# Seven half-size products for the last batch's first MLP product, and a first pair loaded in halves

## The chip, the cores and the metric

The kernel runs on one core of one Trainium2 chip. The metric is the device time of one execution in microseconds (us). It is 278.86 us before the change: the median of three runs that lie between 278.41 and 279.77.

A core has five engines that work side by side, each through its own instructions in order: TensorE (PE in the profile; PEld is its loading of weights), VectorE (DVE), ScalarE (ACT), GpSimd (POOL) and SyncE (SP), which here only issues transfers. They wait for each other by semaphores. PE writes its results to PSUM, a memory of eight banks; DVE and ACT read them there. Everything else lies in SBUF.

## The reference

Four batches of 768 positions go through an attention with 8 heads of 64 columns and then through a mixing layer with an MLP.

```python
# attention: blocks of 64 keys, each query keeps its 3 best blocks and its own
k_rep = k.reshape(B, H, n_blocks, block, D).mean(axis=3)
gate_scores = einsum('bhsd,bhnd->bhsn', q, k_rep)        # causal by blocks
sel = top 3 blocks of gate_scores, and the own block
attn = softmax(scale * q @ k.T, masked by sel and causality)
x = attn @ v                                             # (B, 768, 512)
# mixing
u = x + real(fft(fft(x, axis=1), axis=2))
un = (u - mean(u)) / sqrt(var(u) + 1e-6)
out = u + maximum(un @ w_ch1, 0) @ w_ch2                 # 512 -> 2048 -> 512
```

## The kernel before, in words

The eight heads of a batch are taken in four pairs, so there are 16 pairs, `P` = 0 to 15, and four batches, `b` = 0 to 3. The text `ORDER` names every step of the program once, as `step:arguments@place`. The `place` picks one of four PSUM tiles of two banks each, or one of a few buffers. A `~` ahead of a step puts it on the other of its two possible engines. The loop at the end walks through `ORDER`, and `WORK` gives the function of each step; the engines take their instructions in just this order. Nothing is rearranged at run time.

A pair's steps: `Lq`, `Lk`, `Lv` load q, k and v (SP). `tq` and `tk` (`a_tp`, L314) turn q and k on PE for pairs 0 to 6; for the first pair `tj` (`b_tp`, L323) turns k's last two of six row tiles. `qc` copies q in full precision, `qs` and `kc` write the f16 copies from which scores are made, `ks` and `kj` sum k by blocks. `g`, `gt`, `gx`, `gl`, `gm` (and `gj`, `tg`, `xg`, `lg`, `mg` for the first pair's second part) make the gate scores, turn them, find the third largest, compare (into `lt`) and turn the mask back (into `mt`). `s` are the scores, `e` the exponentials on ACT (L549), `d` the causal masks on POOL (L555), `v` the product with v, `x` its division by the sums.

A batch's steps: `fs`, `fd`, `f` fold the rows, `y` and `m` are the two transforms, `u` adds them to x (L691). `bn` takes mean and variance of each row tile (L747), `nv` guesses the inverse root, `nr` refines it on POOL, `xu` scales, and `un` turns the result by transposing transfers (L742) into `unT`, 512 columns on 4 x 128 partitions by 768 positions.

The MLP: `w:b,it` (L795) is one of 16 tiles of the first product; it takes four slices of 128 of the 512 inner columns, each by a matmul of 512 and one of 256 positions (L801, L803). `r` is its maximum with 0, into `hT` (L811 on DVE, L813 on ACT). In batches 0 and 1 `c` is the second product (L820) and `o` adds it to `u` (L826).

In batches 2 and 3 (`W7`) the second product is made by seven half-size products in place of eight. `T` makes four sums of parts of `w_ch2` in `w2t`, `S:b,i,n` (`h_comb`, L850) makes four sums of parts of `hT` per tile pair `i`, `p:b,n,st` (`w7_mm`, L863) is product `n` for row tile `st`, accumulated over `i`, and `po` (L886) adds PSUM to one or another quarter of `u`. Only two banks per row tile are used: product `n` goes on top of what the bank holds, and `po` reads the bank between products:

```python
W7_BANK = (0, 1, 0, 1, 1, 0, 0)
W7_FIRST = (True, True, False, True, False, False, False)
W7_OUT = ((0, 0), (0, 0), (0, 1), (1, 1), (0, 1), (1, 1), (1, 0))
```

`od` stores rows of `u`. `consts_first` (L896) issues the first pair's loads, makes the constants, and runs eight matmuls of zeros (L914).

Of the kernel before, what the change touches and what calls it, by code (L numbers as in the profile page):

```python
# [19 lines left out]
S = 768  # L20
# [96 lines left out]
e:3,5@1 d:2,2 x:1 s:3,2@0 e:3,0 Lq:6@0 d:3,5 g:5@1 vc:2 e:3,2 s:3,3@2 gt:5 Lk:6@1 d:2,1 gm:4@0
s:3,1@3 d:3,0 gu:5 s:3,4@1 e:3,3 gx:5 d:2,5 v:2@0 d:3,2 kb:7 LT:0 e:3,1 W:0 Lq:7@1 fs:1,0 ~go:5
e:3,4 s:4,4@2 x:2 d:3,1 s:4,2@3 d:3,3 e:4,4@0 s:4,0@1 d:3,4 gl:5 v:3@0 fs:2,0 gm:5@1 e:4,2 fs:2,1
fs:1,1 e:4,0 s:5,2@2 x:3 s:4,5@3 e:5,2@1 s:4,1@1 fd:2,1 s:4,3@0 fs:3,0 e:4,5 s:5,3@2 fs:3,1 e:4,1  # L120
fd:2,0 s:5,5@3 fd:3,1 e:5,5 tq:6@1 fd:3,0 e:4,3 ~fe:0,3 s:5,0@3 f:0,2 e:5,3 tk:6@0 ~fe:0,0 ~fe:0,2
f:0,0 ~qc:6@0 s:5,4@2 LF:0 f:0,1 fe:0,1 ks:6 e:5,4 y:0,0@1 qs:6 Lv:4@0 f:0,3 e:5,0 Lc:0 pg:0 ks:7
d:4,0 g:6@2 d:4,1 ty:0,0 d:4,2 y:0,1@3 gt:6 Lv:5@1 d:4,5 ~tr:0,0 d:5,2 gu:6 gx:6 Lk:8@2 d:4,3
s:5,1@2 W:1 go:6 gl:6 ~tr:0,1 qc:7@1 m:0,2@1 vc:4 ty:0,1 gm:6@2 d:4,4 kc:6 m:0,0@3 d:5,0 u:0,2@0
d:5,4 e:5,1 Lk:9@1 d:5,3 v:4@0 qs:7 u:0,0@1 xu:0,2 s:6,4@1 xv:0,2 x:4 vc:5 m:0,1@2 kh:7 e:6,4@0
d:5,5 s:6,1@3 u:0,1@2 d:5,1 s:6,3@0 e:6,1 xt:0,2@1 ~xu:0,0 g:7@2 xv:0,0 ~xu:0,1 v:5@3 e:6,3 gt:7
un:0,2 ~gu:7 W:2 ~xv:0,1 xt:0,0@2 s:6,5@1 un:0,0 xt:0,1@0 e:6,5 s:6,0@1 un:0,1 Lq:9@2 s:6,2@2 e:6,0
x:5 w:0,8@0 d:6,0 bn:0,0 w:0,1@1 r:0,8 gx:7 kc:7 go:7 w:0,5@3 gl:7 gm:7@3 K:7 kb:8 w:0,6@0 r:0,5
ks:8 r:0,1 bn:0,3 w:0,3@3 r:0,6 d:6,3 bn:0,5 e:6,2 w:0,12@1 r:0,3 Lq:8@0 s:7,5@0 s:7,0@2 ~r:0,12
e:7,5@1 s:7,4@3 kh:8 e:7,0 s:7,3@0 fs:4,1 w:0,0@1 qc:9@0 e:7,4 Li:0 Lv:6@0 kb:9 e:7,3 w:0,10@2 qs:9  # L130
Lv:7@1 bn:0,1 r:0,0 s:7,1@3 Lk:10@0 r:0,10 ks:9 d:7,3 w:0,11@0 e:7,1 qc:8@1 s:7,2@1 kh:9 ~r:0,11
d:7,1 w:0,7@2 e:7,2 d:6,2 d:7,0 fs:5,1 d:6,4 ~qs:8 g:8@3 X:0 g:9@0 gt:8 w:0,14@1 gu:8 d:7,4 gx:8
r:0,7 d:6,5 ~go:8 kc:9 w:0,9@3 X:1 gl:8 gt:9 gu:9 gm:8@0 d:6,1 d:7,5 w:0,2@2 r:0,14 ~r:0,9 Lk:12@1
d:7,2 vc:7 ~vc:6 gx:9 w:0,13@0 K:8 kc:8 kb:10 w:0,4@1 ~r:0,13 r:0,2 ks:10 v:7@3 r:0,4 ~go:9 gl:9
gm:9@1 K:9 s:8,3@0 x:7 s:8,1@2 v:6@1 e:8,1@1 bn:0,2 e:8,3 s:8,0@3 x:6 d:8,1 w:0,15@2 e:8,0 fs:5,0
fs:6,1 s:9,4@0 fs:7,1 r:0,15 fs:7,0 s:8,2@1 fs:4,0 s:8,4@3 e:9,4@0 fd:7,1 c:0,0,0@2 fs:6,0 fd:6,0
e:8,4 fd:7,0 e:8,2 bn:0,4 s:9,3@0 s:9,1@3 fd:6,1 kc:10 s:9,0@1 Lq:10@1 nv:0 c:0,0,1 ~fe:1,1 f:1,2
nr:0 f:1,3 e:9,3 f:1,1 ~fe:1,2 c:0,1,0 fe:1,0 f:1,0 fe:1,3 kh:10 e:9,1 Lv:9@1 kb:12 Lk:11@2 e:9,0
s:9,5@0 c:0,1,1 ks:12 e:9,5 y:1,0@3 o:0,1 Lq:11@2 qc:10@0 y:1,1@1 ~tr:1,0 o:0,0 qs:10 Lq:12@0
g:10@0 ~tr:1,1 c:0,4,0@2 gt:10 gu:10 kb:11 ty:1,0 d:8,2 d:9,5 gx:10 ty:1,1 d:8,0 m:1,2@0 od:0,1  # L140
d:9,1 Lq:13@1 ~go:10 d:9,0 c:0,5,0 u:1,2@3 vc:9 d:8,3 gl:10 ks:11 s:9,2@3 Lk:13@0 m:1,1@1 qc:11@1
kh:11 kh:12 xu:1,2 s:8,5@0 c:0,5,1 gm:10@2 u:1,1@4 K:10 kc:11 Lv:8@0 od:0,0 qc:12@0 c:0,4,1 e:8,5
e:9,2 ~xv:1,2 un:1,2 bn:1,3 pg:1 d:8,4 xu:1,1 g:12@1 d:9,3 g:11@0 d:8,5 c:0,2,0@3 ~qs:11 gt:11
d:9,4 o:0,5 gu:11 gx:11 od:0,5 xv:1,1 un:1,1 m:1,0@0 o:0,4 ~go:11 ~qs:12 gl:11 c:0,3,0 gt:12
gm:11@3 u:1,0@1 K:11 ~vc:8 c:0,3,1 gu:12 gx:12 xu:1,0 kc:12 d:9,2 v:8@2 o:0,3 ~go:12 ~xv:1,0 un:1,0
s:11,3@1 x:8 s:11,4@0 e:11,3@1 c:0,2,1 Lq:14@2 bn:1,4 e:11,4 bn:1,1 s:10,4@2 o:0,2 s:11,2@1 v:9@0
Lk:14@2 qc:13@1 e:11,2 fs:8,1 w:1,15@3 x:9 e:10,4@0 s:10,0@1 bn:1,5 r:1,15 od:0,3 s:10,2@2 od:0,4
gl:12 s:11,0@0 kb:13 e:10,2 w:1,10@3 Lk:15@1 bn:1,2 e:11,0 w:1,2@2 fs:8,0 e:10,0 ~r:1,10 s:11,1@0
gm:12@0 Lv:11@1 kb:14 K:12 s:10,1@1 e:11,1 w:1,4@3 ks:13 Lv:10@0 r:1,2 fs:9,1 s:10,3@0 e:10,1 ks:14
w:1,6@2 d:10,0 kh:13 ~r:1,4 d:11,2 kh:14 e:10,3 d:11,3 w:1,5@1 qc:14@0 r:1,6 s:10,5@3 w:1,12@0  # L150
~r:1,5 qs:13 e:10,5 kb:15 s:11,5@2 g:13@3 e:11,5 vc:11 g:14@1 r:1,12 gt:13 w:1,13@2 fs:9,0 kc:13
~gu:13 Lv:15@1 d:11,4 gx:13 d:10,2 od:0,2 s:12,0@3 d:11,0 bn:1,0 w:1,9@0 d:10,3 r:1,13 ~go:13
# [24 lines left out]
po:2,0,1 p:2,1,2 u:3,2@4 un:3,1 p:2,1,1 S:2,1,1 po:2,1,2 p:2,1,0 po:2,1,1 S:2,1,3 p:2,2,2 S:2,5,3
# [19 lines left out]
def kernel(  # L197
# [649 lines left out]
    def w2t_at(m, i0, i1):  # L847
        return w2t[m // 2][:, m % 2, i0:i1, :]
# [163 lines left out]
```

## Time and profile before

| | us |
|---|---|
| median of three runs | 278.86 |
| lowest and highest | 278.41, 279.77 |
| the profiled execution's own time | 277.79 |
| its span, first to last instruction | 276.1 |
| PE busy | 267.9 |
| DVE busy | 221.5 |
| ACT busy | 178.3 |
| POOL busy | 107.4 |

The profile is one execution. A row of a list of groups names the source line, the engine, the operation, what it writes and reads, how often it ran, its busy time in us, the mean time of one in ns, and how long the engine was idle ahead of it and for whom. A row of the timeline or of the chain of waits begins with its start and its length in us. A row by stretches has the stretch, its length, and the busy time and number of instructions of PE, PEld, DVE, ACT and POOL, and then the clock that PE was granted (1.00 is all of it), the share of the transfers and GB/s. PE's matmuls overlap in the pipeline: the length of one is longer than the time from one to the next.

### The profile page before, as it was taken

Reading aid. Unit: us, or ns where it says so; the run is one execution under the profiler, and the core shown is the slowest. Engines: PE = TensorE matmul, PEld = TensorE weight load, DVE = VectorE, ACT = ScalarE, POOL = GpSimd, SP = SyncE. Lnnn points to the kernel's source line nnn. Section 1 sums busy time; section 2 is a strip of 40 time slices with the busy share of each in tenths; the row PEclk is TensorE's granted clock in tenths of the full one; section 3 lists DMA queues with packets and bytes.
Section 4 is the critical chain, followed back from the end, with each engine's and each line's share of the span. In section 5 each row is a group of like instructions: output and inputs, shape, how many; then the busy total and the mean of one; then the engine's idle time right before and its main releaser. Section 6 shows DMA issues by size and latency. Waiting matters only on the chain.

```text
span 276.1 us, 7004 instructions
## 1 busy us (share of the span) xinstructions
PE 267.9 (97%) x2660; PEld 181.2 (66%) x2660; DVE 221.5 (80%) x683; ACT 178.3 (65%) x243; POOL 107.4 (39%) x304
## 2 busy tenths in 40 slices
PE   8899989999999999999999999999999999999995
PEld 4566766765576565666665755655766888666884
DVE  1888999998789889899789797879999894307883
ACT  3799999969999759978799687802546310274100
POOL 5155927634783476405976691520100011000000
PEclk9999999999999999999999999999999999999999
DMA  8999999998799999479471202351100412300025
GB/s 190 271 229 235 186 233 207 180 153 151 134 174 189 168 188 194 115 124 234 119 149 29 57 2 78 77 105 51 38 2 0 59 19 68 127 0 2 0 112 194
DMA packets 121138, 33.47 MB, mean 121 GB/s; under 512 B 113616, under 2 KB 118160, under 8 KB 121104
## 3 DMA queue, kind: packets, MB, share of 16 engines
q1 hardware_dynamic: 115872, 28.43, 48.1%
q0 software_dynamic: 3664, 4.19, 9.8%
q10 hardware_dynamic: 1568, 0.39, 0.6%
q8 instruction: 21, 0.34, 0.5%
q14 instruction: 13, 0.11, 0.1%
HBM read 28.55 MB, written 6.29 MB: 126 GB/s over the span
## 4 chain that ended last, share of the span: by engine, by line
PE 81%; DVE 6%; ACT 5%; POOL 2%; issue 2%; SPq 2%; DMA 1%; DVEq 0%; ACTq 0%; POOLq 0%
PE h L801 19%; PE cw L879 13%; PE c L820 12%; PE h L803 9%; PE sc L532 7%; PE av L567 5%; PE tp L320 2%; ACT pt L549 2%; PE yp L639 2%; PE sc L527 2%; PE mx L672 2%; SPq L742 2%; PE mx L673 2%; PE sc L539 1%; PE warmps L914 1%
## 5 line engine op out<-in xcount | busy, mean ns | idle before, releaser
L549 ACT ACTIVATE pt<-sc 128x1024 f16<-128x1024 f32 (+1 forms) x96 | 83.4, 925 | 12.1 <-PE sc L532 8.1
L801 PE MATMUL h<-unT,w 128*128 128x512 f16 x256 | 84.6, 379 | 0.3 <-DMA unT<-x 0.3
L803 PE MATMUL h<-unT,w 128*128 128x256 f16 x256 | 69.7, 272 | 0.0
L813 ACT ACTIVATE hT<-h 128x768 f16<-128x768 f32 x50 | 39.4, 811 | 41.1 <-PE h L803 40.7
L555 POOL TENSOR_SCALAR_AFFINE_SELECT pt<-pt 128x256 f16<-128x256 f16 x96 | 37.4, 413 | 21.0 <-ACT pt L549 19.9
L820 PE MATMUL c<-w_sb,hT 128*128 128x512 f16 x192 | 44.5, 379 | 0.0
L801 PEld LDWEIGHTS <-w 128*128 128x128 f16 x256 | 25.0, 98 | 29.7 <-issue 1.4
L820 PEld LDWEIGHTS <-hT 128*128 128x128 f16 x192 | 18.3, 98 | 20.3 <-issue 0.5
L253 POOL TENSOR_SCALAR_AFFINE_SELECT qk<-mt 32x160 f16<-32x160 f16 x72 | 23.9, 353 | 18.2 <-DVE mt L504 16.7
L803 PEld LDWEIGHTS <-w 128*128 128x128 f16 x256 | 25.0, 98 | 3.6
L532 PE MATMUL sc<-qk 96*128 96x512 f16 (+3 forms) x144 | 26.1, 305 | 0.0
L567 PEld LDWEIGHTS <-pt 128*128 128x128 f16 x672 | 22.3, 97 | 3.2 <-ACT pt L549 0.7
L567 PE MATMUL av<-v,pt 128*128 128x65 f16 x672 | 23.2, 193 | 0.3 <-ACT pt L549 0.3
L253 POOL TENSOR_SCALAR_AFFINE_SELECT qk<-q 64x768 f16<-64x768 f32 (+1 forms) x15 | 12.3, 822 | 22.8 <-ACT q L239 15.3
L886 DVE SCALAR_TENSOR_TENSOR u<-cw,rt,u 128x256 f32<-128x256 f32 x35 | 16.6, 480 | 4.7 <-PE cw L879 4.1
L879 PEld LDWEIGHTS <-s 128*128 128x128 f16 x192 | 18.8, 98 | 2.2
L532 PEld LDWEIGHTS <-qk 96*128 96x128 f16 x144 | 13.1, 98 | 7.8
L811 DVE TENSOR_SCALAR hT<-h 128x768 f16<-128x768 f32 x14 | 13.3, 956 | 4.0 <-PE h L803 3.9
L879 PE MATMUL cw<-w2t,s 128*128 128x256 f16 x144 | 16.4, 273 | 0.0
L250 DVE TENSOR_TENSOR s<-hT,hT 128x384 f16<-128x384 f16 x16 | 5.4, 354 | 13.4 <-ACT hT L813 13.3
L250 DVE TENSOR_TENSOR x<-av,rcp 128x768 f16<-128x768 f32 x16 | 15.3, 958 | 0.6
L879 PEld LDWEIGHTS <-hT 128*128 128x128 f16 x144 | 14.1, 98 | 2.0
(155 smaller groups left out, 457.2 us busy)
## 6 DMA issues: line engine op xcount, KB each, us to landing
nat<-in_v_dram SPq DMA_DIRECT2D x16, 384.0 KB, 4.6
out_dram<-u SPq DMA_DIRECT2D x20, 256.0 KB, 2.4
nat<-in_k_dram SPq DMA_DIRECT2D x36, 96.0 KB, 3.4
nat<-in_q_dram SPq DMA_DIRECT2D x36, 96.0 KB, 2.9
nat<-in_q_dram SPq DMA_DIRECT2D x13, 192.0 KB, 3.7
nat<-in_k_dram SPq DMA_DIRECT2D x13, 192.0 KB, 3.9
w_sb<-in_moe_w_ch_dram POOLq DMA_DIRECT2D x2, 1024.0 KB, 11.2
w<-in_moe_w_ch_dram POOLq DMA_DIRECT2D x2, 768.0 KB, 7.1
```

The costliest lines, as they stand in the source:

```text
L250: (eng or nc.vector).tensor_tensor(out=out, in0=in0, in1=in1, op=op)
L253: nc.gpsimd.affine_select(out=out, in_=in_, pattern=[[0, i] for i in n], base=0, channel_multiplier=0, compare_op=ALU.is_ge, fill=0.0)
L532: nc.tensor.matmul(ps[:, e, co:co + q1 - q0], qk[0:96, e, 1, 128 * jt:128 * jt + 128], qk[0:96, e, 0, q0:q1], start=True, stop=True)
L549: nc.scalar.activation(out=d["pt"][:, o:o + 2 * n].rearrange("p (e c) -> p e c", e=2), in_=d["sc", i][:, :, 0:n], func=AF.Exp, scale=0.125)
L555: nc.gpsimd.affine_select(out=dg, in_=dg, pattern=[[0, 2], [1, 128]], base=0, channel_multiplier=-1, compare_op=ALU.is_ge, fill=0.0)
L567: nc.tensor.matmul(av[:, e, 66 * st:66 * st + 65], pt[:, co:co + 128], vv[:, e, jt, 0:65], start=(cnt == 0), stop=(cnt == 20))
L801: nc.tensor.matmul(hp[:, 0:512], w1s, unT[:, dt, 0:512], start=(dt == 0), stop=(dt == NDT - 1))
L803: nc.tensor.matmul(hp[:, 512:768], w1s, unT[:, dt, 512:768], start=(dt == 0), stop=(dt == NDT - 1))
L813: nc.scalar.activation(out=hT, in_=hp, func=AF.Relu)
L820: nc.tensor.matmul(c_ps[b, g[0]][:, st - g[0], :], h_t[b, it][:, 128 * st:128 * (st + 1)], w2_sb[:, it, :], start=(it == 0), stop=(it == N ...
L879: nc.tensor.matmul(o, x, y, start=(i == 0 and W7_FIRST[n]), stop=(i == 7), skip_group_check=True)
L886: nc.vector.scalar_tensor_tensor(out=o, in0=c_ps[b, "w", st][:, W7_BANK[n], 0:256], scalar=rt_t[b][:, kt:kt + 1], in1=o, op0=ALU.mult, op1 ...
```

## The change

It has four parts.

First, the last batch's first product (`W6 = 3`) uses the same scheme of seven as the second ones. The steps `w:3,*` and `r:3,*` go. The weights' 16 tiles are taken as 8 pairs `i`, `i + 8`, the inner columns as two halves, the positions as two halves of 384. `wa` makes four sums of quarters of `w_ch1` (in free parts of `qk_s` and of the tiles of `w2t`), `ub` four sums of quarters of `unT`. `k:i,n` is product `n` of pair `i`, two matmuls of 384 positions. `zc` copies an unfinished bank to SBUF in full precision (ACT or DVE), `za` adds the other bank and a copy (DVE), `zm` takes the maximum of that sum (ACT or DVE), `zr` takes the maximum of a bank that is finished. Since the halves of the positions come out swapped, `half` swaps them again in the second product.

Second, the variance of batches 2 and 3 is no longer made by `bn` on DVE. `mn` takes the mean from the row sums that `u` leaves, and `sq` sums the squares on ACT.

Third, the first pair's q and k are loaded in two parts, four row tiles and two, k first: eight transfers in place of four, six of them from SP. `tn` turns q's last two row tiles as `tj` does k's, and `qn` and `qm` copy that part. There are seven matmuls of zeros in place of eight, from a smaller buffer.

Fourth, `ORDER` is new in all its parts. Among others, some `S` and `wa` are on POOL now, batch 3's mixing stands earlier among the products of batch 2, and the first `k` stand between the `p` of batch 2.

```diff
+W6 = 3
+W6_A = ((0, 2), (2, 4), (4, 8))
 ORDER = """
...
+tk:0@1 Lk:1@1 tn:0@2 ks:0 Lq:1@1 tj:0@3 ~qn:0@0 tq:0@0 kd:0 kj:0 Lq:2@2 qc:0 gj:0@2 tg:0 ~qs:0
+g:0@3 Lk:2@2 xg:0 tk:1@0 ~qm:0 gt:0 kc:0 og:0 gu:0 gx:0 ks:1 Lk:3@0 ~go:0 tq:1@2 lg:0 gl:0 mg:0@0
...
+S:2,2,3 xu:3,0 un:3,0 k:0,0@0 po:2,2,1 p:2,3,2 S:2,0,3 p:2,3,1 po:2,3,2 ~S:2,5,2 k:0,1 p:2,4,2
+po:2,2,0 zc:0,0 po:2,3,1 p:2,3,0 po:2,4,2 ub:0 od:2,2 p:2,4,1 S:2,6,2 ub:1 p:2,5,2 po:2,4,1 za:0,0
...
+zm:3,0 k:2,4 k:3,3 zr:1 ~zm:1,1 ~S:3,0,1 k:3,5 za:2,2 zc:4,0 k:1,4 zc:3,2 k:5,0@3 za:4,0 ~S:3,0,2
+zm:2,2 k:5,1 za:1,2 k:3,6 zc:5,0 k:4,2 ~zm:4,0 za:3,1 k:6,0@2 zc:4,1 k:6,1 za:5,0 zr:3 k:4,3
...
+    def b_tq(P):
+        pairs[P]["tpn"] = ps = pst([128, 256], f"tpn_{P}")
+        src = nat[P, 0].rearrange("p st e d -> p st (e d)")
+        for st in range(4, NST):
+            nc.tensor.transpose(ps[:, 128 * st - 512:128 * st - 384], src[:, st, :], id32)
...
+    def n_mean(b, kp):
+        sm = st_t[b][2][:, 2 * kp:2 * kp + 2]
+        nc.vector.tensor_scalar(out=sm, in0=sm, scalar1=-1.0 / DM, scalar2=None, op0=ALU.mult)
+
+    def n_square(b, kt):
+        nc.scalar.activation(out=x_t[b][:, kt, :], in_=u_t[b, kt // 2][:, kt % 2, :], func=AF.Square,
+                             bias=st_t[b][2][:, kt:kt + 1], accum_out=st_t[b][0][:, kt, 1:2])
...
+    def w6_mm(i, n):
+        if (i, "p") not in w6:
+            w6[i, "p"] = pst([128, 2, 512], f"k{i}_{W6}")
+        o = w6[i, "p"][:, W7_BANK[n], 0:384]
+        x = (lambda: w6_w(i, 0, 0), lambda: w6_w(i, 0, 1), lambda: w6_sum(1, i, i + 1),
+             lambda: w6_sum(0, i, i + 1), lambda: w6_sum(3, i, i + 1), lambda: w6_sum(2, i, i + 1),
+             lambda: w6_w(i, 1, 1))[n]()
+        y = (lambda: w6_b(0, 0), lambda: w6_b(1, 0), lambda: w6_t(1), lambda: w6_t(0), lambda: w6_b(1, 1),
+             lambda: w6_t(2), lambda: w6_t(3))[n]()
+        for d in range(2):
+            nc.tensor.matmul(o, x[:, d, :], y[:, d, :], start=(d == 0 and W7_FIRST[n]), stop=(d == 1),
+                             skip_group_check=True)
+
+    def w6_keep(i, j):
+        conv(pick(nc.scalar, nc.vector), w6_copy(i, j), w6[i, "p"][:, 0, 0:384], None)
+
+    def w6_relu(i):
+        hp, h = w6[i, "p"][:, 0, 0:384], w6_h(i, 1, 0)
+        if pick(0, 1):
+            nc.vector.tensor_scalar(out=h, in0=hp, scalar1=0.0, scalar2=None, op0=ALU.max)
+        else:
+            nc.scalar.activation(out=h, in_=hp, func=AF.Relu)
+
+    def w6_add(i, j):
+        tt(w6_tmp(i, j), w6[i, "p"][:, 1, 0:384], w6_copy(i, (0, 2, 1)[j]), ALU.add)
+
+    def w6_max(i, j):
+        h, t = w6_h(i, *((0, 0), (1, 1), (0, 1))[j]), w6_tmp(i, j)
+        if pick(0, 1):
+            nc.vector.tensor_scalar(out=h, in0=t, scalar1=0.0, scalar2=None, op0=ALU.max)
+        else:
+            nc.scalar.activation(out=h, in_=t, func=AF.Relu)
...
     def consts_first():
...
+        for h in (slice(0, 4), slice(4, NST)):
+            for who in (1, 0):
+                src = (q, k)[who]
+                for e, eng in ((0, nc.sync), (1, nc.sync if h.start else nc.scalar)):
+                    eng.dma_start(nat[0, who][:, h, e, :],
+                                  src[0, e].rearrange("(st p) d -> p st d", p=128)[:, h, :])
...
-        for _ in range(8):
-            nc.tensor.matmul(wps, wsrc[:, 0:128], wsrc, start=True, stop=True)
+        for _ in range(7):
+            nc.tensor.matmul(wps.rearrange("p (r c) -> p r c", c=128), wsrc, wsrc.rearrange(
+                "p (r c) -> p r c", r=1).to_broadcast([128, 4, 128]), start=True, stop=True)
```

## The prediction

> **What bounds the kernel now.** I read the page's head and chain of waits first, then the last 90 us by stretches, then single rows.
>
> ```profile
> span 276.1 us, 7004 instructions
> PE 267.9 (97%) x2660; PEld 181.2 (66%) x2660; DVE 221.5 (80%) x683; ACT 178.3 (65%) x243; POOL 107.4 (39%) x304
> ...
> PE 81%; DVE 6%; ACT 5%; POOL 2%; issue 2%; SPq 2%; DMA 1%; DVEq 0%; ACTq 0%; POOLq 0%
> ...
> L801 PE MATMUL h<-unT,w 128*128 128x512 f16 x256 | 84.6, 379 | 0.3 <-DMA unT<-x 0.3
> ```
>
> TensorE (PE) is busy for 267.9 of 276.1 us and carries 81% of the chain, with almost no idle time ahead of the `h` products. A change must shorten PE's own work, or it must win at a place where PE waits. The stretches are batch 2's first MLP product with batch 3's mixing, batch 2's second product, batch 3's first product, batch 3's second product:
>
> ```profile
> 187.40:214.40 27.00, 26.93 (x184) 17.55 (x185) 25.38 (x67) 13.92 (x20) 1.09 (x1) 1.00 0.05 20
> 214.40:233.40 19.00, 19.00 (x177) 17.02 (x175) 15.46 (x44) 2.51 (x4) 2.54 (x11) 1.00 0.27 44
> 233.40:254.20 20.80, 20.80 (x133) 12.81 (x131) 6.35 (x16) 9.30 (x12) 0.00 (x0) 1.00 0.14 52
> 254.20:276.10 21.90, 18.61 (x168) 16.15 (x165) 15.28 (x43) 0.81 (x1) 0.00 (x0) 1.00 0.27 97
> ```
>
> ```profile
> 272.84 0.48 DVE L886 SCALAR_TENSOR_TENSOR qk<-cw,rt,qk 128x256 f32<-128x256 f32 x1 [0.39 <-PE cw L879]
> ```
>
> From 187.4 on PE is as good as never free, until its last product ends at about 272.8; the last eviction and store then take 3.3 us, before and after the change. In the third stretch VectorE (DVE) works 6.4 and ScalarE (ACT) 9.3 of 20.8 us, so batch 3's first product is bound by PE alone, and the others have room there. In the first stretch DVE has 1.6 us of room in 27.0.
>
> **1. The seven products (all `k` steps).** Now each of 16 output tiles takes four pairs of matmuls, of 512 and 256 columns, so 64 pairs:
>
> ```profile
> 233.50 0.38 PE L801 MATMUL h<-unT,w 128*128 128x512 f16 x1
> ...
> 233.83 0.38 PE L801 MATMUL h<-unT,w 128*128 128x512 f16 x1
> ```
>
> ```profile
> 255.34 17.48 PE cw L879 x160
> ```
>
> A pair begins 0.33 us after the one before it (233.50, 233.83); over the third stretch it is 20.8 us / 64 = 0.325 us for 768 columns. 256 columns take 17.48 / 160 = 0.109 us, so 512 take 0.216. A 384-column matmul should lie in the middle, at 0.1625. The change needs 8 tiles x 7 products x 2 = 112 of them: 18.2 us. **Term 1: 18.2 - 20.8 = -2.6 us**, all on the path, as the stretch has no other bound. Each has its own weight load, as now.
>
> **2. What pays for it.** A tile now leaves PSUM by one maximum per 768 columns (16 in all). After it: 24 copies (`zc`, 21 on ACT), 24 adds (`za`, all DVE), 24 maxima (`zm`, 15 ACT and 9 DVE) and 8 maxima from PSUM (`zr`, 7 ACT), each 384 columns. None of these forms is in the trace; the nearest rows:
>
> ```profile
> L813 ACT ACTIVATE hT<-h 128x768 f16<-128x768 f32 x50 | 39.4, 811 | 41.1 <-PE h L803 40.7 <-ACT hT L813 0.3
> ```
>
> ```profile
> 244.10 3.62 ACT L813 ACTIVATE hT<-h 128x768 f16<-128x768 f32 x5 [0.43 <-PE h L803]
> ```
>
> ```profile
> L886 DVE SCALAR_TENSOR_TENSOR u<-cw,rt,u 128x256 f32<-128x256 f32 x35 | 16.6, 480 | 4.7 <-PE cw L879 4.1
> L250 DVE TENSOR_TENSOR x<-av,rcp 128x768 f16<-128x768 f32 x16 | 15.3, 958 | 0.6
> L747 DVE BATCH_NORM_STATS2 bst<-u 128x6 f32<-128x512 f32 x22 | 14.8, 674 | 0.0
> ```
>
> ```profile
> L724 DVE TENSOR_SCALAR x<-u,nm 128x512 f16<-128x512 f32 x5 | 2.6, 512 | 0.1
> ```
>
> ```profile
> 254.81 0.35 DVE L250 TENSOR_TENSOR s<-hT,hT 128x384 f16<-128x384 f16 x1
> ```
>
> ```profile
> 259.54 0.62 DVE L250 TENSOR_TENSOR s<-hT,s 128x384 f16<-128x384 f16 x2
> ```
>
> ACT takes 0.811 for 768 columns, and five in a row 3.62, so 0.72 each; 384 columns fewer are 0.32 less at 1.2 columns per ns (768 columns at that rate are 0.64, the rest is fixed), so 0.40 to 0.49. DVE reads 768 columns of PSUM in 0.958, which is 0.80 at 0.96 columns per ns and 0.156 fixed; 384 give 0.556, and in a row less, since two 384-column `s` take 0.62 together where one alone takes 0.35 (0.27 for the second): 0.47 to 0.556. The lower ends are for queues that run without a gap. `zm` on DVE: 0.512 for 512, so 0.31 to 0.41. `po` is 0.40 to 0.48.
>
> The tight stretch in the new order runs from product `k:0,6` to `k:7,4`: 45 products of 0.325 and three `p` of 8 x 0.109, so 17.2 us of PE. In it stand on DVE 20 `za`, 9 `zm`, 2 `zc`, 1 `zr`, 3 `po` and 6 `S`: 9.4 + 2.8 + 0.9 + 0.5 + 1.2 + 1.6 = 16.4 us at the lower ends, 20.0 at the upper ones (11.1 + 3.7 + 1.1 + 0.6 + 1.4 + 2.1). On ACT 16 `zc`, 12 `zm`, 7 `zr`: 35 x 0.40 = 14.0 to 17.2. So PE is the bound by 0.8 us at the lower ends, DVE by 2.8 at the upper ones. I take the lower ends, for a queue that is 95% full has its next instruction waiting, with 0.3 us of stalls. The first ten products run between batch 2's `p` steps, where 21 x 0.87 + 10 x 0.325 = 21.5 us of PE stand over some 19 us of DVE (20 `po`, 12 `S`, 4 `ub`, 3 `wa`, 4 from PSUM, and 2 us for batch 3's last rows): covered.
>
> **3. Inputs of the products.** Batch 3's turns move up: `un:3,2` is now issued while `p:2,1` runs, and `k:0,0` follows six `p` later.
>
> ```profile
> 182.27 2.52 SPq L742
> 184.84 2.50 DMA unT<-x
> ```
>
> Two turns hold SP's queue for 2.52 us and land 2.50 later. `xu:3,2` ends about 2.7 us after the start of `p:2,0,2` (two `p`, then `po:2,0,0` and 0.5 for itself); 2.5 + 2.5 more are 7.8, and `k:0,0` stands after nine `p` = 7.8: 0 to 0.5, taken 0.2. `un:3,0` waits behind these on SP and feeds `ub:0`, which stands on DVE ahead of `po:2,4,1` and three more evictions; by the same steps DVE waits there some 1.5 us and PE 0.2, because the next `p` into that bank comes three products later. Stores go behind the turns on SP; nobody waits for them until the end. **Term 2: 0.3 + 0.2 + 0.2 = +0.7 us** of stalls (0 to 3.2).
>
> **4. Weight sums, deviations, `S` on POOL.**
>
> ```profile
> L250 DVE TENSOR_TENSOR w2t<-w_sb,w2t 128x2048 f16<-128x2048 f16 x2 | 2.4, 1212 | 0.0
> ```
>
> ```profile
> L555 POOL TENSOR_SCALAR_AFFINE_SELECT pt<-pt 128x256 f16<-128x256 f16 x96 | 37.4, 413 | 21.0 <-ACT pt L549 19.9
> ```
>
> ```profile
> L253 POOL TENSOR_SCALAR_AFFINE_SELECT v<-nat 128x768 f16<-128x768 f32 x13 | 12.3, 946 | 0.2
> ```
>
> ```profile
> L250 DVE TENSOR_TENSOR sd<-x x32: 316/350/731, 25.7 to 186.9; 128x384 f16<-128x384 f16 x32
> ```
>
> Twelve `wa` sums: at 1.212 per 2048 elements the four sums are 4 x 1.2 = 4.8 us, five pieces of 512 of them on POOL. Twelve `bn` (0.674 and an aggregate) leave DVE, some 9 us, and become twelve squares of 512 columns on ACT, each at most the 0.72 of the 768-column maximum, 8.6 us; ACT has 13 us free in the first stretch. 19 of 64 `S` go to POOL, which is idle there. A two-input POOL operation of this size is not in the trace; one-input forms bound it at 0.41 (256) and 0.95 (768), so 0.55, and below one end nothing excludes 0.35. POOL has over 10 us free in each stretch, so these are hidden. Queued behind `wa:0,0` and `wa:1,0` on POOL are the last masks of pairs 14 and 15, for which `v:14` and `v:15` wait; a `c` half of 8 x 0.216 = 1.73 us stands on PE ahead of each: 0, or up to 0.9 if that cover is gone. DVE's relief shows in no PE wait: 0. Term 3: 0 (-0.5 to +0.9).
>
> **5. The head.**
>
> ```profile
> 1.31 3.59 PE warmps L914 x8
> 4.90 2.15 PE tp L320 x10
> ```
>
> ```profile
> 7.98 0.51 PE g L433 x8
> ```
>
> ```profile
> 10.48 0.23 DVE mt L376
> ```
>
> ```profile
> 8.74 1.53 PE L320 MATMUL tp<-id,nat 128*128 128x128 f32 x12
> ```
>
> ```profile
> 0.83 0.45 SPq L903 DMA_DIRECT2D nat<-in_q_dram  x1
> ...
> 1.94 1.14 SPq L304 DMA_DIRECT2D nat<-in_q_dram  x2
> 3.12 4.13 SPq L304 DMA_DIRECT2D nat<-in_k_dram  x4
> ```
>
> ```profile
> DMA to landing us min/median/max: 3.2/3.8/4.4
> ```
>
> Now the first mask (10.48 + 0.23 = 10.7) comes from warm-up matmuls to 4.9, transposes at 0.215 to 7.05, the sum, and the gating. After it 7 warm-ups of 0.45 end 0.6 earlier, and `k`'s first four transposes run under the remaining loads. But `tn` stands second and needs the last of eight loads. SP issues six of them at about 0.5, the last from 3.3; it lands at most 3.2 later (the shortest of the row, for three times its bytes), and I allow 0.8 less: 5.7 to 6.5. Then eight transposes of 0.215, the copy of `q32` (0.7) and `g` (0.51) end at 8.6 to 9.4, against 8.5. DVE has part of the maxima done by then, but the new order puts the sum of pair 1 (768 columns of PSUM, 0.96 as above) ahead of `lt`. So the first mask lands between 10.0 (loads at 4.9, sum in a gap) and 11.6. SP's four issues in 4.13 us show that the ninth load waits for an early one to land: pair 1's loads start at 4.0 instead of 1.9, land by about 9, and are needed at 9: covered, with nothing left. ScalarE and VectorE issue the same work, only reordered. **Term 4: 0 (-0.7 to +0.9)**, the middle.
>
> Ten transposes took 2.15 us here and twelve 1.53 from 8.74 on: PE ran at half its rate until about 7, 5.7 us after its first matmul. The Trainium skill (TensorE: Matmul & The Clock Gate, Part 1) lets the clock double after some 3.4 us of sustained activity and fall back after an idle window; the trace agrees on the doubling, not on the 3.4. By that rule the shorter warm-up and the pause ahead of `tn` could keep PE at half rate for a window more, which would put term 4 at its bad end and the time at 277.9.
>
> **Sum.** -2.6 + 0.7 + 0 + 0 = -1.9 us. The profiled execution took 277.79 us for its 276.1 span, so 275.9 after; the median of the runs is 278.86, 1.07 above it, so **277.0**. Under 0.5% (1.4 us) a difference is no change here: 277.5 to 280.3.
>
> **Rivals.**
>
> *VectorE becomes the bound of the last first product.* At the upper prices of part 2 it needs 20.0 us under 17.2 of PE: 2.8 of stalls instead of 0.3, so 279.5, no change. For it: pieces are short, and each `za` waits for a matmul and a ScalarE copy, so queues may run with gaps. Against: back-to-back `s` overlap. 0.18.
>
> *The hand-offs decide: slower.* Every tile's two PSUM banks are read while the sum in them is unfinished: three copies and two adds per tile stand between a product and the next into that bank, 40 in all, and PE takes its products in order. At a mean PE wait of 0.07 us each the gain of 2.6 is gone, over 0.1 it is slower by 0.5%; a late copy delays its add, the next product and the next tile's bank. At 0.12, 40 x 0.12 = 4.8 us take the place of the 0.7: 281.1. For it: both other engines are at 81 to 95% there. Against: some nine products, 2.9 us, stand between two into one bank, over a copy of 0.49. 0.24.
>
> *POOL and DVE hold each other up.* The `sd` row has 0.350 in the middle and 0.731 at worst, with POOL at work beside it. 24 POOL operations that could each cost DVE 0.38 are 9 us; the ten in the tight stretch 3.8, less 0.8 of room, so 3.0 more: 280.0. Against: the median row shows nothing. The Trainium skill (SBUF — State Buffer, Who interferes with whom) says that a VectorE instruction with two SBUF inputs and a GpSimd one that reads SBUF block each other for a whole instruction; by that rule, the trace's 0.731 is such a block and `za`, with one input in PSUM, is exempt. 0.06.
>
> **Chances.** The forecast holds with 0.52, in 275.2 to 277.9 (all terms at good ends: -2.6 - 0.5 - 0.7 = -3.8 gives 275.1). Range 275.0 to 281.1: outside lie half of the hand-off case and a few in a hundred below, together under 0.2. Faster 0.53 (most of the forecast, and a better head), no change 0.18 (the VectorE case and parts of two others), slower 0.29.
>
> **What would show it.** Right: `k` matmuls of 384 columns every 0.1625 us; PE without idle time from `k:0,6` to the last `p`; first to last `k` with its `p` shorter by 2.6 us in sum; `za` at 0.56, DVE near 95% there. Wrong: idle PE ahead of `k` released by `za` (VectorE) or `zc` (ScalarE), `p:3,2` waiting for `S`; a first mask well past 11.5; PE waiting for turns ahead of `k:0,0`.

## The result and the profile after

The changed kernel takes 279.52 us (median of 20 runs, 278.04 to 280.9), the kernel before 278.00 beside it (20 runs): a ratio of 1.0051, 95% interval 1.0032 to 1.007. It is slower by 1.4 us; the forecast was faster by 1.9, as a ratio 0.993 (its 277.0 was reckoned from three runs with a median of 278.86). So 3.3 us are missing.

The head of the page of the changed kernel; its own time is 279.54 us:

```profile
span 277.8 us, 7100 instructions
...
PE 267.2 (96%) x2643; PEld 179.0 (64%) x2643; DVE 234.8 (85%) x698; ACT 193.4 (70%) x298; POOL 128.5 (46%) x322
...
PE 76%; DMA 6%; ACT 4%; issue 4%; DVE 3%; POOL 3%; SPq 2%; DVEq 0%; ACTq 0%
```

The chain of waits in time, from the first `p` of batch 2 on (start, length, engine, tile and line), and the tight stretch (columns as in the prediction):

```profile
218.57 7.86 PE cw L1032 x72
...
240.16 13.29 PE k L957 x80
...
258.18 15.73 PE cw L1032 x144
...
273.94 0.49 DVE qk L1039
```

```profile
239.20:258.20 19.00, 19.00 (x127) 12.19 (x126) 18.14 (x45) 15.34 (x36) 9.31 (x10) 1.00 0.01 2
```

The end of the kernel is much as forecast: from the first `p` to the last matmul's end, 273.94 - 218.57 = 55.4 us, PE has no wait that the timeline lists, only a few short pauses, to which the section on the prediction comes back. In the kernel before, the chain has there:

```profile
214.45 2.62 PE cw L879 x24
```

272.84 - 214.45 = 58.4 us, with `m:3,2` in it, which the new order makes earlier (8 matmuls of 256 columns, 0.87). The products are 58.4 - 0.9 - 55.4 = 2.1 us quicker. The loss is all ahead of 218.57: the first `p` starts 4.1 us later than before, 0.9 of it for `m:3,2`. The waits of PE there that are new or longer, or come later, in PE's timeline of the changed kernel:

```profile
5.87 0.41 PE L350 MATMUL tpn<-id,nat 128*128 128x128 f32 x2 [1.06 <-DMA nat<-in_q_dram]
...
12.12 0.37 PE L573 MATMUL sc<-mt,indz 64*128 64x96 f16 x8 [0.21 <-DVE mt L410]
...
65.86 0.38 PE L842 MATMUL h<-unT,w 128*128 128x512 f16 x1 [0.69 <-DVE hT L852]
...
164.00 1.17 PE L601 MATMUL av<-v,pt 128*128 128x65 f16 x33 [0.76 <-DVE u L725]
...
192.44 0.38 PE L842 MATMUL h<-unT,w 128*128 128x512 f16 x1 [0.85 <-DMA unT<-x]
```

The second is no longer than the wait for the first mask in the kernel before (0.32 ahead of 10.75); it comes 1.4 us later. The third stands behind a load of 11.34 us in the chain, and no other profile of this case has a wait of 0.3 us or more at that place, so I put it down to this execution. The last two have causes that the trace shows. Ahead of 164.00, VectorE's timeline and then GpSimd's:

```profile
159.89 2.75 DVE L815 TENSOR_SCALAR rs<-rs 128x6 int32<-128x6 int32 x1
162.55 0.68 DVE L725 SCALAR_TENSOR_TENSOR u<-mx,x 128x512 f32<-128x512 f32 x1
```

```profile
157.65 1.71 POOL L270 TENSOR_SCALAR_AFFINE_SELECT qk<-q 64x768 f16<-64x768 f32 x2
159.43 0.41 POOL L589 TENSOR_SCALAR_AFFINE_SELECT pt<-pt 128x256 f16<-128x256 f16 x1
159.78 0.18 POOL L661 COPY gone<-fg 1x4 f16<-1x4 f16 x1
159.92 0.40 POOL L589 TENSOR_SCALAR_AFFINE_SELECT pt<-pt 128x256 f16<-128x256 f16 x1
160.28 0.89 POOL L270 TENSOR_SCALAR_AFFINE_SELECT v<-nat 128x768 f16<-128x768 f32 x1
161.13 1.48 POOL L589 TENSOR_SCALAR_AFFINE_SELECT pt<-pt 128x256 f16<-128x256 f16 x4
```

`nv:1`'s third operation, on six numbers per partition, takes 2.75 us; it ends when GpSimd's run ends, which has no pause from 159.43 on (161.13 + 1.48 = 162.61). In the kernel before the same one took this (shortest, middle, longest of two, in ns):

```profile
L774 DVE TENSOR_SCALAR rs<-rs x2: 173/263/353, 90.4 to 151.2; 128x6 int32<-128x6 int32 x2
```

It stands ahead of `u:2,0`, which empties the PSUM tile that `v:13` takes. Ahead of 192.44, the issue queue of the kernel before and of the changed one:

```profile
171.53 3.17 SPq L742 DMA_TRANSPOSE unT<-x  x2
...
179.09 2.50 SPq L742 DMA_TRANSPOSE unT<-x  x2
...
182.27 3.83 SPq L742 DMA_TRANSPOSE unT<-x  x2
```

```profile
181.89 8.71 SPq L776 DMA_TRANSPOSE unT<-x  x6
```

Batch 2's six turns went out in three pairs, as `bn` had each pair's statistics. With the squares on ScalarE, between its exponentials, they stand in a row from 181.89 on, and the first product waits for the last. The last of the six `bn` in the kernel before, and the first and last of the six squares in the changed one:

```profile
176.79 0.66 DVE L747 BATCH_NORM_STATS2 bst<-u 128x6 f32<-128x512 f32 x1
```

```profile
166.61 0.72 ACT L784 ACTIVATE x<-u,sm 128x512 f16<-128x512 f32 x1
...
181.76 0.71 ACT L784 ACTIVATE x<-u,sm 128x512 f16<-128x512 f32 x1
```

### The profile page after: what moved, and what is told of

Its sections match the earlier page's. It is cut to its first block, busy times and chain, and to the rows that moved or that the text cites. A ratio compares the mean times of both kernels' runs of the same rounds, so it can differ in the third digit from the quotient of the medians.

```text
span 277.8 us, 7100 instructions
## 1 busy us (share of the span) xinstructions
PE 267.2 (96%) x2643; PEld 179.0 (64%) x2643; DVE 234.8 (85%) x698; ACT 193.4 (70%) x298; POOL 128.5 (46%) x322
## 4 chain that ended last, share of the span: by engine, by line
PE 76%; DMA 6%; ACT 4%; issue 4%; DVE 3%; POOL 3%; SPq 2%; DVEq 0%; ACTq 0%
PE h L842 14%; PE cw L1032 13%; PE c L861 12%; PE sc L566 7%; PE h L844 7%; PE k L957 7%; PE av L601 5%; DMA nat<-in_k_dram 4%; ACT pt L583 4%; PE tp L337 2%; PE yp L673 2%; POOL pt L589 2%; DMA unT<-x 1%; SPq L316 1%; PE g L475 1%
## 5 line engine op out<-in xcount | busy, mean ns | idle before, releaser
L842 PE MATMUL h<-unT,w 128*128 128x512 f16 x192 | 63.8, 379 | 1.6 <-DMA unT<-x 0.9
L844 PE MATMUL h<-unT,w 128*128 128x256 f16 x192 | 52.3, 272 | 0.0
L861 PE MATMUL c<-w_sb,hT 128*128 128x512 f16 x192 | 43.9, 379 | 0.0
L854 ACT ACTIVATE hT<-h 128x768 f16<-128x768 f32 x37 | 29.1, 809 | 20.1 <-PE h L844 20.1
L842 PEld LDWEIGHTS <-w 128*128 128x128 f16 x192 | 18.7, 97 | 22.4 <-DVE u L867 1.3
L566 PE MATMUL sc<-qk 96*128 96x512 f16 (+3 forms) x144 | 26.8, 306 | 0.0
L844 PEld LDWEIGHTS <-w 128*128 128x128 f16 x192 | 18.8, 98 | 3.4 <-issue 0.9
L439 ACT CAST qk<-nat 64x768 f16<-64x768 f32 x18 | 14.9, 830 | 0.3
L561 PE MATMUL sc<-qk 64*128 64x512 f16 (+3 forms) x112 | 14.5, 306 | 0.5 <-DVE x L267 0.2
L725 DVE SCALAR_TENSOR_TENSOR u<-mx,x 128x512 f32<-128x512 f32 x22 | 14.1, 687 | 0.4 <-PE mx L707 0.4
```

Of the source, the lines that this page charges most:

```text
L566: nc.tensor.matmul(ps[:, e, co:co + q1 - q0], qk[0:96, e, 1, 128 * jt:128 * jt + 128], qk[0:96, e, 0, q0:q1], start=True, stop=True)
L842: nc.tensor.matmul(hp[:, 0:512], w1s, unT[:, dt, 0:512], start=(dt == 0), stop=(dt == NDT - 1))
L844: nc.tensor.matmul(hp[:, 512:768], w1s, unT[:, dt, 512:768], start=(dt == 0), stop=(dt == NDT - 1))
L854: nc.scalar.activation(out=hT, in_=hp, func=AF.Relu)
L861: nc.tensor.matmul(c_ps[b, g[0]][:, st - g[0], :], h_t[b, it][:, 128 * st:128 * (st + 1)], w2_sb[:, it, :], start=(it == 0), stop=(it == N ...
```

## The experiments

My theory after the result: the seven products gain what was forecast, and the new order ahead of them loses it in a few waits. Rivals: such waits would be swallowed by the next anyway; or the products themselves carry the loss. Every ratio below is to the kernel before on the same chip, with its 95% interval; the changed kernel has 1.0051.

### Which stretch: the old order up to a point, the new one behind it

The order's text is the old one up to the step named, then the new one without what is done; head and loads are the old ones in all four.

```diff
-ORDER = new
+ORDER = old up to w:2,7 (v:9, v:4, v:0) + what is left of new
```

> The old order, the old whole loads and the old statistics of batch 2 up to the first product of batch 2 (near 190 us), then the new order with the seven-product scheme; the weight sums that stood before that point follow the first maxima of batch 2, on VectorE. Theory A (the seven products gain what was forecast, and everything that the new order does before them loses about 3 us): 276.6 against 279.5 of the changed kernel, 1.4 below the kernel before. Theory B (the loss before the products would be swallowed by waits in them anyway, so the seven-product tail itself is worth nothing): 278 to 279.5.

> The changed kernel with the old order and whole loads up to v:9 (118 us in the changed kernel's trace), the new order behind it. There the changed kernel lies 1.5 us behind the kernel before in matmul work done. Theory A: 278.0, that is 1.5 below the changed kernel. Theory B (such a lag is taken up later): 279.5, no difference from the changed kernel.

> The changed kernel with the old order and whole loads up to v:4 (some 57 us), the new order behind it, so with the late load of k for pair 8 still in it. The lag there is 0.3 us at most. Theory A: 279.2. Rival, that the head's 1.3 us come back at the end: 278.2.

> The changed kernel with only the head undone: whole loads of the first pair, eight matmuls of zeros, the old order up to v:0 (some 18 us). The head costs 1.3 us at v:0 and 0.3 at 58 us in the two traces. Theory A (only what is left at 58 us counts): 279.2 to 279.5. Rival (the first matmuls' delay goes through to the end): 278.2.

Measured: 278.16 (1.0015, 1.0006 to 1.0024), 287.03 (1.0335), 282.15 (1.0162), 278.70 (1.0033, 1.002 to 1.0045). The two in the middle tell nothing about the changed kernel: a seam between two orders makes waits of its own, 5.05 us ahead of 129.60 in the one, 1.20 and 1.11 near 54 us in the other. The first lies at the edge of theory B; but it too has a seam wait, 1.6 us at 198.5, without which it would be near the 276.6 of theory A, so it decides nothing. The last is 0.5 us better than the changed kernel, with intervals that overlap, and lies between its theory and its rival.

### VectorE behind GpSimd

```diff
-e:13,2 nv:1 pg:2 ... u:2,0@0 ... u:2,2@2 nr:1
+e:13,2 pg:2 ... u:2,0@0 ... u:2,2@2 nv:1 nr:1
```

> The changed kernel with one step moved: nv:1, the three small operations on VectorE of which one took 2.75 us at 159.9 us, stands behind u:2,2 in place of ahead of u:2,0. Theory A (that operation held up u:2,0 and so v:13, 0.76 us of idle time of TensorE, which comes back): 278.7. Rival (the turned rows of batch 2 are late anyway, so TensorE waits for them at 192 us the longer): 279.4, no change.

Measured: 278.35, 1.0004 (0.9987 to 1.0021), that is 1.3 us better than the changed kernel. The operation at its new place, where GpSimd has nothing to do, and PE's row of `v:13`, without a wait:

```profile
162.45 0.17 DVE L814 TENSOR_SCALAR rs<-rs 128x6 int32<-128x6 int32 x1
```

```profile
161.55 1.44 PE L600 MATMUL av<-v,pt 128*128 128x65 f16 x42
```

Theory A holds. That the gain is more than the wait of 0.76 us is not shown, given the two intervals. A second pair of runs differs by the place of `nv:1` alone: old_to_v0 (1.0033), whose PE still waits 0.76 us for `u:2,0`, and guess_old_head further below (1.0006), where that wait is gone. They lie 0.75 us apart, just the wait.

The next kernel was to show the seven products alone. It shows the mechanism instead.

```diff
+ORDER = old up to p:2,3,2, with ~wa (GpSimd) behind r:2 ... + tail of new
```

> The seven-product scheme alone in the old order: head, loads, bn statistics and all of batch 2 as in the kernel before, up to p:2,3,2 (near 222 us); from there the new order's tail. Nine of the twelve weight sums run on GpSimd beside the first product of batch 2, where GpSimd had nothing. Theory A (the products are worth their 2.6 us and the loss lies in the rest of the new order): 275.9 to 276.5, a ratio of 0.993 to 0.995 to the kernel before. Theory B (the products bring waits of their own, or GpSimd's sums slow VectorE there): 277.5 to 278.5.

Measured: 286.28, 1.0306 (1.0283 to 1.033). VectorE, GpSimd and PE:

```profile
197.89 6.82 DVE L266 TENSOR_TENSOR w2t<-w_sb,w2t 128x2048 f16<-128x2048 f16 x1
```

```profile
197.07 1.15 POOL L266 TENSOR_TENSOR qk<-qk,w 128x512 f16<-128x512 f16 x1
198.18 1.15 POOL L266 TENSOR_TENSOR qk<-w 128x512 f16<-128x512 f16 x1
199.30 1.14 POOL L266 TENSOR_TENSOR w2t<-w,qk 128x512 f16<-128x512 f16 x1
200.41 2.10 POOL L266 TENSOR_TENSOR qk<-w 128x1024 f16<-128x1024 f16 x1
202.49 1.14 POOL L266 TENSOR_TENSOR qk<-qk,w 128x512 f16<-128x512 f16 x1
203.70 2.02 POOL L266 TENSOR_TENSOR w2t<-w,qk 128x512 f16<-128x512 f16 x1
```

```profile
205.69 0.39 PE L705 MATMUL mx<-fd_sb,tr 128*128 128x256 f16 x1 [4.98 <-DVE tr L257]
```

An operation of 1.2 us takes 6.82, for as long as GpSimd's sums follow one another without a pause (to 203.63), and PE waits 4.98 us. Neither theory had that.

```diff
-~wa ... bn:3,*            (of seven_alone)
+wa  ... mn:3,* sq:3,*     m:3,2 u:3,2 ahead of p:2,0,2
```

> As seven_alone, with the weight sums on VectorE in place of GpSimd, the squares of batch 3 on ScalarE as in the changed kernel (they make room on VectorE), and the last third of batch 3's mixing a little earlier. Theory A (in seven_alone GpSimd's sums, back to back, kept one VectorE operation waiting for 5.6 us; without them the seven products gain 2 us in the old order): 275.8 to 276.6. Theory B (VectorE has no room for the sums in the first product of batch 2): 278 to 279.

Measured: 280.30, 1.0097 (1.007 to 1.0125). PE does not wait in batch 2's first product now (VectorE 24.3 of 27.7 us there, theory B falls), but four times from 216 to 228 us, 0.58 + 0.46 + 0.89 + 1.17 = 3.1 us, for evictions and turns that I had put together by hand. Without them 277.2 would be left, 0.6 above theory A; that is only worked out. Each new place of a step makes a wait somewhere.

```diff
+wa:2,1 wa:0,0 wa:1,0 wa:0,1 wa:3,1   (VectorE, were ~wa on GpSimd; and nv:1 as above)
```

> The changed kernel with nv:1 behind u:2,2, and the five weight sums that were on GpSimd on VectorE. Theory A (each held VectorE up for longer than it takes there, 0.9 against 0.4 us, ahead of the statistics of batch 2, so the turned rows come sooner): 277.3 to 277.7. Rival (VectorE's wait there is hidden): 278.0, as guess_later. Second rival (VectorE is the bound there, and 2.5 us more of work cost): 278.5.

Measured: 278.27, 1.0013 (0.9994 to 1.0032). The first rival: the five sums cost nothing on the path. In the changed kernel's trace seven VectorE operations are held up: 2.75, 1.25, 0.80, 1.06, 1.30, 1.05 and 1.07 us for 0.17, 0.41, 0.16, 0.17, 0.35, 0.35 and 0.35, which makes 7.3 us. The second to fifth are gone without the sums, and PE had not waited behind them.

### The head

```diff
-ORDER = old
+ORDER = new up to v:0 + old   (first pair in halves; no seven products)
```

> The kernel before with the head of the changed one alone: first pair loaded in halves, seven matmuls of zeros, the new order up to v:0; everything behind it as before, with no seven products. Theory A (1.3 us late at v:0, and waits that stand behind it anyway take up most of it): 278.1 to 278.4. Rival (the delay goes through to the end): 279.3. Second rival (it gains, as the first mask's earlier sums suggest): 277.5.

Measured: 279.88, 1.0085 (1.0057 to 1.0113), 2.0 us above the kernel before by the medians and 2.4 by the ratio: the rival, and more. And in the changed kernel, with `nv:1` moved:

```diff
+ORDER = old up to v:0 + new with nv:1 behind u:2,2
```

> The changed kernel with nv:1 behind u:2,2 (as guess_later) and the old head up to v:0 (as old_to_v0). Theory A (both losses are separate and add up: 1.1 and 0.5 us): 277.5, a ratio of 0.9985 to the kernel before. Rival (the head costs what it did in the old order, 2.0 us): 276.0. Second rival (the later wait for the turned rows takes it up): 278.0.

Measured: 277.90, 1.0006 (0.9996 to 1.0016), no better than guess_later: the second rival. So the head loses some 2 us in the old order and between 0 and 0.5 in the new one. In none of these runs does it gain.

### Turns and stores

Four things at once were tried first, and bn for all six row tiles of batch 2:

```diff
+old head; nv:1 behind u:2,2; Lk:8 ahead of Lv:5, W:2 behind un:0,2
+bn:2,* for sq:2,*, xu:2 and un:2 right behind their nv:2
```

> The changed kernel with four things mended: the old head up to v:0; nv:1 behind u:2,2; k of pair 8 loaded ahead of v of pair 5, and the last part of the first weights later; the statistics of batch 2 by bn on VectorE in place of squares on ScalarE, with the scaling and the turns right behind them. Theory A (the four waits are the whole loss and add up: 0.8, 0.76, 0.69 and 0.6 us off 279.4): 276.6. Rival (what one gives the next takes back): 278 to 279.

```diff
+nv:1 behind u:2,2; bn:2,* for sq:2,*, four of them around o:1,1
```

> The changed kernel with nv:1 behind u:2,2, and the statistics of batch 2 by bn on VectorE in place of squares on ScalarE, so that the first four turns of rows are issued some 6 us sooner. Theory A (the six turns in a row from 182 us are what TensorE waits 0.9 us for near 190 us): 277.3. Rival (VectorE's 5 us more of work there cost as much as they bring): 278.0 to 278.5.

Measured: 284.37 (1.0234, 1.021 to 1.0258) and 282.62 (1.0185, 1.0153 to 1.0216). Both lose the wait near 190 us and make a larger one: 5.70 us at 171.0, ScalarE's `xu:2` waiting for VectorE ahead of the exponentials; 3.10 at 173.4, `o:1` queued behind four `bn`. They say how much stands on those queues, not what the turns cost. So smaller:

```diff
-od:3,3 ... od:2,4 ... od:2,3 ... od:2,1
+od:2,4 od:2,3 od:2,1 od:3,3     (on guess_old_head)
```

> As guess_old_head, with three stores of batch 2's rows issued ahead of batch 3's first, not between them. In the changed kernel's trace the last three stores are issued at 273.79, 274.28 and 274.78 us, though their rows are ready by 274.43, and between the last matmul's end and the span's end lie 3.9 us, against 3.3 before. Theory (the store queue is that late): 277.4, that is 0.5 less than guess_old_head. Rival (the end is set by the last row tile anyway): 277.9.

```diff
-mn:2,0 sq:2,0 sq:2,1 ... nv:2,0 ... xu:2,0 ... un:2,0
+gm:15 bn:2,0 bn:2,1 nv:2,0 ... e:14,3 xu:2,0 un:2,0 ... o:1,0 od:1,1 od:1,0   (on guess_old_head)
```

> As guess_old_head, with bn on VectorE for the first two row tiles of batch 2 alone, in the 3.3 us in which VectorE waits at 164 us, so two of the six turns are issued near 169 in place of 182 us. Theory (TensorE's wait of 1.0 us near 190 us goes to the 0.2 that the kernel before had): 277.1. Rival (the last turn is late for its own statistics, not for the five ahead of it): 277.9.

> Both: stores_early and bn_two. Theory (they add up): 276.6, a ratio of 0.996 to the kernel before, below both kernels. Rival (no gain): 277.9.

```diff
+both, and the five wa on VectorE
```

> As both_mends, with the five weight sums on VectorE in place of GpSimd. Theory (each no longer keeps VectorE from an operation beside it): 276.4. Rival (VectorE's own 2 us more cost as much, as guess_no_pool_sums gave nothing): 276.6, or 277 with VectorE late for the turns.

Measured: 277.43 (0.9989, 0.9975 to 1.0003), 277.78 (0.9998, 0.9981 to 1.0014), 277.70 (0.9995, 0.9982 to 1.0008), 277.44 (0.9997, 0.9979 to 1.0015). The stores may hold 0.5 us, not more than the measurement tells apart, and the traces do not show it: from the last matmul's end to the span's end it is 3.5 us in guess_old_head and 3.4 in stores_early. They do not add up with the turns; for bn_two and both_mends the rivals hold, and all_mends lies above its theory and its rivals. The trace of both_mends says why the turns bring nothing there: the wait near 190 us is gone, a new one stands in PE's row at 177.84, and SP's queue and VectorE show what is ahead of it:

```profile
177.84 1.46 PE L868 MATMUL c<-w_sb,hT 128*128 128x512 f16 x6 [1.57 <-DVE u L725]
```

```profile
168.92 2.52 SPq L776 DMA_TRANSPOSE unT<-x  x2
171.49 1.05 SPq L880 DMA_DIRECT2D out_dram<-u  x2
```

```profile
176.47 0.69 DVE L725 SCALAR_TENSOR_TENSOR u<-mx,x 128x512 f32<-128x512 f32 x1 [4.75 <-DMA out_dram<-u]
```

The two turns stand on SP ahead of the stores `od:1,1` and `od:1,0`, and `u:2,1` takes the buffer that these empty. One step moved back:

```diff
-xu:2,0 un:2,0 ... o:1,0 od:1,1 od:1,0
+xu:2,0 ... o:1,0 od:1,1 od:1,0 un:2,0
```

> As all_mends, with the two early turns of batch 2 issued behind the two stores of batch 1's rows, not ahead of them. In all_mends u:2,1 waited at 171.6 us for those stores (it takes their buffer), 4.1 us on VectorE and 1.2 us on TensorE near 177 us, where the wait near 190 us had gone. Theory (the turns only moved the wait into the store's way; behind the stores both waits are gone): 276.2 to 276.5, a ratio of 0.995 to the kernel before. Rival (TensorE finds the next wait): 277.4.

> As turns_behind_stores, but the five weight sums stay on GpSimd as in the changed kernel. Theory (they hold VectorE up, 3 us in all, near 170 to 180 us, now with nothing in between that hides it): 276.8 to 277.2. Rival (hidden): 276.3, the same.

Measured: 275.91 (0.9925, 0.9904 to 0.9946) and 275.98 (0.9919, 0.9902 to 0.9937). The second differs from both_mends by this one place in the issue queue, and is 2.1 us better. In its trace PE does not wait near 177 or 190; the chain from the first `p` on begins and ends

```profile
215.34 7.86 PE cw L1039 x72
...
254.95 15.73 PE cw L1039 x144
270.71 0.48 DVE qk L1046
```

and the sums on GpSimd cost nothing (the rival of turns_pool_sums). Both beat both kernels: 2.0 us below the one before, 3.6 below the changed one. The end lasts 270.71 - 215.34 = 55.4 us, as in the changed kernel, and the first `p` starts 0.9 us later than in the kernel before (214.45), which is `m:3,2`. So ahead of the first `p` nothing is lost any more, and the 2.0 us are the products' 2.1.

## Why the prediction was wrong

- *Term 1, the products, -2.6.* Right, with its price. Where nothing holds PE up, eight `k` matmuls take 251.99 - 250.69 = 1.30 us, 0.1625 each. The 80 of the chain take 13.29, 0.166 each, because PE pauses for about 0.1 us at a few places: 247.26 + 4 x 0.1625 is 247.91, the next begins at 248.03, when ScalarE's copy ends. Four such pauses (ahead of 244.63, 248.03, 249.39 and 255.59) make 0.4 us. With them the 112 take 18.6 against 20.8, -2.2; measured over the whole end, -2.1.

```profile
247.26 0.81 PE L957 MATMUL k<-unT,w 128*128 128x384 f16 x4
248.03 0.81 PE L957 MATMUL k<-uns,qk 128*128 128x384 f16 x4
...
250.69 1.46 PE L957 MATMUL k<-uns,qk 128*128 128x384 f16 x8
251.99 0.49 PE L957 MATMUL k<-unT,w2t 128*128 128x384 f16 x2
```

```profile
247.50 0.48 ACT L256 COPY w<-k 128x384 f32<-128x384 f32 x1 [0.21 <-PE k L957]
```

- *The evictions of part 2, and with them the two rivals of that stretch.* Right, and so is the reason for the lower ends. `za` lasts 0.55 and `zc` on ScalarE 0.48, the upper ends, and `zm` on ScalarE 0.52, above its own; but in a row they start closer together, as the lower ends have it: 0.47 from one VectorE operation to the next here, and 0.27 behind a `zm` (248.15 to 248.42).

```profile
249.25 0.55 DVE L267 TENSOR_TENSOR w_tr<-k,w 128x384 f32<-128x384 f32 x1
249.72 0.55 DVE L258 COPY fs_sb<-k 128x384 f32<-128x384 f32 x1
250.18 0.46 DVE L267 TENSOR_TENSOR s<-hT,s 128x384 f16<-128x384 f16 x1
```

  So VectorE has work for 18.14 of 19.00 us and PE stays the bound. The pauses, 0.4 us in all, came out near the 0.3 of stalls; the rival of the hand-offs had 4.8.
- *Term 2, +0.7.* Its 0.3 of stalls measured 0.4; its two 0.2 for inputs measured nothing (no wait ahead of `k:0,0`). But the step asks only when batch 3's turns go out. The same question for batch 2, whose statistics the change moved too, was not asked: 0.85 us of PE's wait in place of 0.27, and with the queue's place behind it up to 2 us (both_mends against turns_pool_sums).
- *Term 3, at 0: the step that failed.* "DVE's relief shows in no PE wait: 0" and "ACT has 13 us free in the first stretch" compare busy time with room. But batch 2's six squares do not run in that stretch, which begins at 187.4: they run from 166.61 to 182.5, between exponentials. What mattered was when the result comes: the last square starts at 181.76, the last `bn` started at 176.79 (a part of the 5.0 us between them is the delay that the changed kernel had by then), and the six turns end at 190.6 on SP's queue instead of 186.1. GpSimd's price was short too, 0.91 to 0.95 us for an `S` of 384 elements instead of 0.55, though the five weight sums, 1.15 to 1.32 each, cost nothing on the path.
- *The third rival, POOL and DVE.* The mechanism is there, in another place and size. I priced ten operations at 0.38 each in the tight stretch; in the trace it is one operation of `nv:1`, 2.6 us longer than alone, with GpSimd's masks and its copy of v beside it, and it costs 0.75 to 1.3 us of the time. The Trainium skill (SBUF — State Buffer, Who interferes with whom) says more there than I used: copies, casts and `tensor_scalar` of VectorE, with one input, can contend with GpSimd too when they run in a mode that takes both ports. The trace agrees for the integer `tensor_scalar`, as far as its length tells. The page's rule that the second to issue is blocked until the first finishes does not cover what is seen: here VectorE waits through a run of several.
- *Term 4, the head, at 0.* "ScalarE and VectorE issue the same work, only reordered" was the error in general: the order is the change. The first mask is ready at 12.1, outside the 10.0 to 11.6. The causes named there are in the trace: the last of eight loads ends the wait at 5.87 (5.7 to 6.5 forecast), the sum of pair 1 stands ahead of `lt`. They alone do not carry it past the range: with the same head it comes at 11.16 in guess_later, 11.28 in guess_no_pool_sums and 11.36 in halves_alone. The rest is the granted clock, which fell in this execution (the fields are the stretch, its length and PE's busy time, then, in the first row, the other engines', and last clock, transfers and GB/s):

```profile
7.00:10.50 3.50, 2.79 (x23) 1.94 (x24) 2.69 (x17) 1.41 (x3) 0.11 (x1) 0.61 1.01 229
```

```profile
7.80:11.20 3.40, 3.40 (x27) 0.50 1.03 233
```

  The Trainium skill (TensorE: Matmul & The Clock Gate, Part 1), which the prediction weighed, puts such a fall behind an idle window of about 3.4 us. Here the pauses ahead of it are shorter, 1.06 us and 0.78 at 7.71. And the traces of halves_alone and guess_later have a pause of 1.28 us at this place and 1.00 in the row from 7.00 to 10.50, so the length of the pause alone does not decide; halves_alone is 2 us slower in that execution too. Half the clock for 3.4 us is a mean of 0.994 over the kernel. The mean clock is 0.994 or less in 5 of the changed kernel's 20 runs and in 11 of the 30 of guess_later, guess_no_pool_sums and halves_alone, but in none of the 75 of old_to_w2, old_to_v0, stores_early, bn_two, both_mends, all_mends and the last two kernels, which have the old head. The list does not tell where in a run it fell.

Together: from the changed kernel to the last one 0.0132 of 278 us are won back, 3.7 us: 0.75 to 1.3 by `nv:1`, 2 by the turns and their place, the rest by head and stores together, which the runs do not part. That is what the forecast missed. The last kernel stands 2.0 below the one before, where the sum of -1.9 had put the changed one; its order differs, so it shows that the products are worth what was forecast, not that the prediction had the order right.

Still open: why the head costs 2.0 us in the old order and next to nothing in the new one. A part of it may be a wait of 0.99 us that PE has in halves_alone at 25.77 for ScalarE's copy of q and k (the kernel before waits 0.47 at 25.71, for VectorE); that was not tried.

## What to carry to other kernels

When an order is rewritten, the steps whose work is unchanged are the ones to cost: for each engine and for the issue queue, look at what now stands ahead of an instruction for which the bounding engine waits, and when its input comes, not how busy the engine is. A step that moves from one engine to another changes what is queued behind it and ahead of it, and a transfer issued early can hold up a store whose buffer is wanted next. Keep small VectorE operations on the path away from stretches in which GpSimd works without a pause.

## What the hardware showed that I had not expected

- VectorE is kept out for a whole run of GpSimd operations: 2.75 us for 0.17, 6.82 for 1.2. In the one case that shows it, it came in where GpSimd's rows have a gap, of 0.07 us in seven_alone (203.63 to 203.70), and GpSimd's next sum then took 2.02 instead of 1.14.
- A long wait costs PE its clock as well: 0.62 in the 4 us after the 3.10 us of guess_bn (from 173.40 on). By stretches in seven_alone, after its wait of 4.98 us:

```profile
205.00:209.00 4.00, 3.31 (x11) 0.50 0.02 4
209.00:213.00 4.00, 4.00 (x23) 0.87 0.00 0
```

  (the fields after the stretch and its length are PE's busy time, the granted clock, the transfers): half the clock until about 210, and the 0.87 is the mean over the second stretch. 3.31 x 0.50 + 4.00 x 0.13 = 2.2 us of PE's work are lost beyond the wait itself.
